# An SSD scan with a maxout FFN on one core: operand parts in three steps, queued steps two per unit, the maxima's parts on VectorE, and the last output in two stages

## The chip, the core and the metric

The kernel runs on one core of a Trainium2 chip. The core has TensorE (matrix products into PSUM), VectorE, ScalarE and GpSimd, each with its own queue of instructions worked off in order, and SyncE, whose queue here issues transfers. The engines wait for one another by semaphores. The metric is the device time of one execution in microseconds (us). In the profile PE is TensorE, PEld its loading of weights, DVE is VectorE, ACT is ScalarE, POOL is GpSimd and SP is SyncE.

## The reference

For 4 batches, 8 heads, 768 positions, head width 32 and state width 16, the first half is a scan with decays, written in chunks of positions:

```python
log_a = np.log(np.clip(a, 1e-06, 1.0))
cum = np.cumsum(la, axis=-1)                       # la: log_a of one chunk
L = np.exp(cum[..., :, None] - cum[..., None, :]) * causal
y_intra = ((C_c @ B_c^T) * L) @ x_c
y_inter = (C_c @ state) * np.exp(cum)
state = exp(sum(la)) * state + (B_c * exp(cum[-1] - cum))^T @ x_c
```

The heads are then put side by side (3072 tokens of 256 values) and go through a maxout layer and an output layer:

```python
h = np.maximum(np.maximum(x @ w1, x @ w2), x @ w3)  # 256 -> 768
return (h @ w_out).astype(np.float32)               # 768 -> 256
```

All is float32, and float32 accuracy is wanted.

## The kernel before

**Tiling.** The kernel takes 128 positions of all four batches at a time: six blocks (c = 0 to 5) of 512 tokens. For each block the scan makes the scores (L559, one group for batches 0 and 1 and one for batches 2 and 3), weights them by the decays (`scan_weight`, L567, on VectorE), and adds the old state's part (L582) and the block's own (L595). The decays are exponentials on ScalarE (L460, four heads per `part`), of a table L that comes by DMA and is masked on GpSimd (L453). `scan_c` (L501) makes C's transposed form, `scan_cd` (L512) the decayed one, from a bank of PSUM that it thereby sets free.

**The layer.** The three weights of the first layer, in 9 pieces of 256 columns, and the output weight, in 3 pieces, are 12 "weights". They arrive as raw words (`fetch`), are decoded into floats (`decode`: L208 and L217 on ScalarE, L209 and L212 on VectorE, L218 on GpSimd; `sign`: L221 on VectorE), and block 0 uses these whole floats (L657, L761). Blocks 1 to 5 use another form: every operand is split into parts, a high one, a low one and a scaled difference, in a type with faster products, and three products stand for one: the difference's product (L701 for the first layer), scaled by −KAPPA in the bank by ScalarE (L687), and then the high and the low part's products on top of it (L718). `weight_parts` makes a weight's parts, `scan_y` those of y, and `hidden` those of a maximum: high part on ScalarE (L636), low part by a subtraction on GpSimd (L637; on VectorE for the last two maxima only), difference on VectorE (L630).

**Units.** A block's first layer is 18 units (9 weights k, two halves g). A unit makes L718 for its bank and opens the bank two units ahead (L701, L687), in a ring of four banks; VectorE copies the result (L723) or takes the maximum (L725). A maximum is done after three weights; its parts are started one unit later and finished another unit later (`after`). With all six maxima of a block done, the "down" products with the output weight (L766) follow, listed in `downs`: for each half of the batches first Y (the difference's products, then scaled) and then X (the other two). They are issued in the middle of the next block's units, at places that the tables X1 to X3 and Y1 to Y3 set with a "D".

**Order.** The program is written out by hand; each engine gets its instructions in the order of the calls. Steps of the scan that would hold up VectorE are put in a list, `later`, and `pop(1)` after each unit releases one of them. In the loop over block 0's 18 groups (n) and in block 1's units, the weights are decoded and split step by step; W1 says which split starts at which k. The parts of the last three weights are finished at the end of block 1 (`finals`), because the buffers are those that block 0's down products read.

**Pools.** Scores, transposes, y, states and outputs share a ring of four banks (`att_bank`).

Of the kernel before, what the change touches and what calls it, by code (L numbers as in the profile page):

```python
# [20 lines left out]
def kernel(  # L21
# [218 lines left out]
    def weight_parts(k):  # L240
# [6 lines left out]
        def last():  # L247
# [13 lines left out]
    splitting = []

    def split(k=None):

        for step in splitting:
            step()
        del splitting[:]
        if k is not None:
            a, b, *splitting[:] = weight_parts(k)
            a()  # L270
            b()
# [420 lines left out]
    AHEAD = 2  # L692
# [13 lines left out]
    def unit():  # L706
# [35 lines left out]
    downs, outs, finals = [], {}, {}  # L742
# [4 lines left out]
    def down_next():  # L747
# [9 lines left out]
        for b in bs:  # L757
# [13 lines left out]
            if what == "X" and c == NC - 1:  # L771
                put(c, o, (b,))
        if what == "Y":
            down_scaled(o)
        elif c < NC - 1 and (c > 0 or bs[0] % 2):
            put(c, o, (2 * a, 2 * a + 1))

    def put(c, o, bs):

        ob = ffn.tile([P, 2, DM], FP32, tag="ob", name="ob")  # L780
        part = slice(bs[0] % 2, bs[-1] % 2 + 1)
        nc.scalar.activation(  # L782
            ob[:, part], o[:, part], AF.Copy, scale=(1.0 + TAU) ** 2 if c else 1.0)
        (nc.scalar if c == NC - 1 else nc.sync).dma_start(
            out=out.rearrange("(b s) m -> s b m", s=S)[c * P:(c + 1) * P, bs[0]:bs[-1] + 1],
            in_=ob[:, part])
# [99 lines left out]

    for n in range(NF * 3):
# [85 lines left out]
    for c in range(1, NC):  # L973
# [3 lines left out]
        for k in range(NW):  # L977
            unit()
            pop(1)
            if c == 1:  # L980
                if k < 2:
                    sign()
                if k == 0:
                    decode()
                if k < 4:
                    split(W1[k])
                elif W1[k]:
                    *steps, finals[W1[k]] = weight_parts(W1[k])
                    for step in steps:
                        step()  # L990
# [21 lines left out]
            pop(1)  # L1012
# [13 lines left out]
        if c == 1:  # L1026
# [35 lines left out]
```

## Time and profile before

| | us |
|---|---|
| median of 3 runs (341.5 to 345.76) | 342.2 |
| the profiled execution | 341.14 |
| its span, first to last instruction | 339.4 |

| engine | busy us | share of the span | instructions |
|---|---|---|---|
| TensorE | 294.3 | 87% | 2054 |
| VectorE | 177.2 | 52% | 264 |
| ScalarE | 183.3 | 54% | 409 |
| GpSimd | 126.2 | 37% | 112 |

The mean granted clock of TensorE is 0.94 of full speed. Busy shares are means over stages that differ, so the stages have to be read one by one; a wait is the bracket at a row's end, with the time that the engine stood idle before the instruction and what it waited for. A row's time is counted from the span's start.

### The profile page before, as it was taken

Reading aid. Unit: us, or ns where it says so; the run is one execution under the profiler, and the core shown is the slowest. Engines: PE = TensorE matmul, PEld = TensorE weight load, DVE = VectorE, ACT = ScalarE, POOL = GpSimd, SP = SyncE. Lnnn points to the kernel's source line nnn. Section 1 sums busy time; section 2 is a strip of 40 time slices with the busy share of each in tenths; the row PEclk is TensorE's granted clock in tenths of the full one; section 3 lists DMA queues with packets and bytes.
Section 4 is the critical chain, followed back from the end, with each engine's and each line's share of the span. In section 5 each row is a group of like instructions: output and inputs, shape, how many; then the busy total and the mean of one; then the engine's idle time right before and its main releaser. Section 6 shows DMA issues by size and latency. Waiting matters only on the chain.

```text
span 339.4 us, 5409 instructions
## 1 busy us (share of the span) xinstructions
PE 294.3 (87%) x2054; PEld 222.0 (65%) x2054; DVE 177.2 (52%) x264; ACT 183.3 (54%) x409; POOL 126.2 (37%) x112
## 2 busy tenths in 40 slices
PE   7899949969698499699799999799999899999765
PEld 4664324646465387498478798477897576887564
DVE  2758766965336434421837722767614467426810
ACT  2965956847847646625447755466845144245221
POOL 4346695669744701900507401434303032012100
PEclk9999987999959789979969999989999799999979
DMA  7979799989070003902703902600000000010001
GB/s 86 281 236 318 132 161 273 199 167 167 32 91 3 0 2 101 234 8 78 77 2 100 210 3 86 69 2 2 0 33 32 0 2 1 2 62 0 2 0 62
DMA packets 105049, 28.13 MB, mean 83 GB/s; under 512 B 75328, under 2 KB 101952, under 8 KB 105024
## 3 DMA queue, kind: packets, MB, share of 16 engines
q1 hardware_dynamic: 104144, 27.14, 39.6%
q10 hardware_dynamic: 880, 0.66, 0.6%
q8 instruction: 16, 0.26, 0.3%
q14 instruction: 9, 0.07, 0.1%
HBM read 24.54 MB, written 3.24 MB: 82 GB/s over the span
## 4 chain that ended last, share of the span: by engine, by line
PE 53%; DVE 16%; issue 13%; POOL 11%; ACT 5%; POOLq 0%; ACTq 0%
PE up L718 13%; PE o L766 12%; PE up L701 9%; PE up L657 5%; PE s L559 4%; DVE h L630 4%; POOL wd L250 3%; POOL wp L256 3%; DVE m L723 3%; DVE m L725 3%; POOL L L453 2%; PE y L595 2%; DVE L L567 2%; ACT L L460 2%; DVE six L623 1%
## 5 line engine op out<-in xcount | busy, mean ns | idle before, releaser
L718 PE MATMUL up<-six,wp 128*128 128x512 f32 x360 | 102.1, 412 | 0.4 <-ACT up L687 0.3
L637 POOL TENSOR_TENSOR h<-m,h 128x512 fp32r<-128x512 f32 x28 | 35.9, 1286 | 150.0 <-ACT h L636 149.6
L718 PEld LDWEIGHTS up<-six,wp 128*128 128x128 f32 x360 | 71.5, 200 | 18.5 <-ACT up L687 2.7
L725 DVE TENSOR_TENSOR m<-m,up 128x512 f32<-128x512 f32 x60 | 41.0, 684 | 80.7 <-PE up L718 80.3
L687 ACT ACTIVATE up<-up 128x512 f32<-128x512 f32 x90 | 51.2, 582 | 54.6 <-PE up L701 54.5
L701 PE MATMUL up<-six,wd 128*128 128x512 f32 x180 | 62.0, 432 | 6.4 <-DVE six L630 5.8
L460 ACT ACTIVATE L<-L,ncums 128x128 f32<-128x128 f32 x160 | 50.2, 390 | 3.5 <-POOL L L453 3.5
L701 PEld LDWEIGHTS up<-six,wd 128*128 128x128 f32 x180 | 33.1, 201 | 19.3 <-DVE six L630 8.0
L559 PE MATMUL s<-six,six 32*128 32x256 f32 x192 | 26.2, 456 | 16.9 <-DVE L L567 7.2
L723 DVE COPY m<-up 128x512 f32<-128x512 f32 x30 | 20.6, 688 | 34.1 <-PE up L718 33.3
L630 DVE SCALAR_TENSOR_TENSOR h<-h,h 128x512 fp32r<-128x512 f32 x30 | 33.6, 1121 | 7.7 <-POOL h L637 7.6
L559 PEld LDWEIGHTS s<-six,six 32*128 32x128 f32 x192 | 15.0, 203 | 26.4 <-issue 12.3
L766 PE MATMUL o<-wp,h 128*128 128x256 f32 x240 | 31.2, 287 | 1.0 <-ACT ob L782 1.0
L657 PE MATMUL up<-six,w 128*128 128x512 f32 x64 | 31.3, 635 | 0.7 <-ACT wp L258 0.5
L766 PEld LDWEIGHTS o<-wp,h 128*128 128x128 f32 x240 | 30.4, 195 | 1.7 <-ACT ob L782 1.4
L567 DVE TENSOR_TENSOR L<-s,L 128x512 f32<-128x512 f32 x46 | 30.4, 680 | 0.0
L766 PE MATMUL o<-wd,h 128*128 128x256 f32 x120 | 18.8, 304 | 7.4 <-DVE h L630 6.4
L453 POOL TENSOR_SCALAR_AFFINE_SELECT L<-L 128x1024 f32<-128x1024 f32 x20 | 24.7, 1259 | 0.0
L766 PEld LDWEIGHTS o<-wd,h 128*128 128x128 f32 x120 | 17.3, 207 | 9.5 <-DVE h L630 7.3
L657 PEld LDWEIGHTS up<-six,w 128*128 128x128 f32 x64 | 12.4, 203 | 16.9 <-issue 12.6
L636 ACT ACTIVATE h<-m 128x512 fp32r<-128x512 f32 x30 | 18.7, 624 | 8.8 <-DVE m L725 8.8
L218 POOL TENSOR_TENSOR six<-six 128x512 uint32<-128x512 uint32 x12 | 15.3, 1271 | 20.9 <-DVE six L212 10.5
(93 smaller groups left out, 294.4 us busy)
## 6 DMA issues: line engine op xcount, KB each, us to landing
L<-cums SPq DMA_DIRECT2D x10, 1024.0 KB, 8.9
rb<-in_moe_w_dram SPq DMA_DIRECT2D x9, 512.0 KB, 6.4
raw_x<-in_x_dram SPq DMA_DIRECT2D x6, 512.0 KB, 10.9
out_dram<-ob SPq DMA_DIRECT2D x10, 256.0 KB, 2.1
raw_B<-in_B_dram SPq DMA_DIRECT2D x6, 256.0 KB, 4.5
raw_C<-in_C_dram SPq DMA_DIRECT2D x6, 256.0 KB, 6.4
rb<-in_moe_w_out_dram SPq DMA_DIRECT2D x3, 512.0 KB, 5.1
E<-cums SPq DMA_DIRECT2D x40, 32.0 KB, 2.2
```

The lines of the kernel that those rows point to most:

```text
L453: nc.gpsimd.affine_select(out=Ls[c][:, b], in_=Ls[c][:, b], pattern=[[0, NH], [1, P]], compare_op=ALU.is_ge, fill=MASKED, base=0, channel_ ...
L460: nc.scalar.activation(L[:, b, h], L[:, b, h], AF.Exp, bias=ncum[c][:, b * NH + h:b * NH + h + 1], scale=1.0)
L559: nc.tensor.matmul(out=s[:, i].rearrange("j g i -> j (g i)"), lhsT=st["BT"][rows, b], rhs=st["CT"][rows, :, b], start=(i == 0), stop=True, ...
L567: nc.vector.tensor_tensor(out=M, in0=s, in1=M, op=ALU.mult)
L630: nc.vector.scalar_tensor_tensor(out=out, in0=lo.bitcast(FP32), scalar=-1.0 / TAU, in1=hi.bitcast(FP32), op0=ALU.mult, op1=ALU.add)
L637: (nc.vector if soon else nc.gpsimd).tensor_tensor(out=lo, in0=src, in1=hi.bitcast(FP32), op=ALU.subtract)
L657: nc.tensor.matmul(out=bank, lhsT=whole[3 * (f // 2) + i][:, k, f % 2 * P:(f % 2 + 1) * P], rhs=yT[0][:, k], start=(k == 0), stop=(k == KD ...
L687: nc.scalar.activation(bank, bank, AF.Copy, scale=-KAPPA)
L701: nc.tensor.matmul(out=o, lhsT=weight_part(k, 2, kk, cols), rhs=yT[c][2][:, kk], start=(kk == 0), stop=(kk == KD - 1), skip_group_check=True)
L718: nc.tensor.matmul(out=o, lhsT=weight_part(k, j, kk, cols), rhs=yT[c][j][:, kk], start=False, stop=(kk == KD - 1 and j == 1), skip_group_c ...
L725: nc.vector.tensor_tensor(out=m[g], in0=m[g], in1=o, op=ALU.max)
L766: nc.tensor.matmul(out=o[:, b % 2], lhsT=hs[f][p][:, tokens(b)], rhs=weight_part(NW + f // 2, p, f % 2, slice(0, DM)), start=(first and p ...
```

## The change

**Weights' parts.** ScalarE now makes both scaled copies of a weight one behind the other (the high part in `lo`'s place, and the high part times TAU in `hi`'s), then GpSimd subtracts, then GpSimd makes the difference. All parts are smaller by TAU than before, and the output's scale, BACK, makes up for it in both layers. The steps are called by number (`split(k, step, ...)`): W0 sets them for weights 0 to 3 in the loop over n, W1 now for weights 4 to 11 in block 1's units (the copies in the unit's first half, the two GpSimd steps in its second); `finals` is gone. The decoding of weights is moved to other n, earlier, and ends in the loop.

**Queued steps.** `pop(1)` after each unit becomes `pop(2)`.

**Maxima.** The subtraction of `hidden` is on VectorE for all 30 maxima, and is made with the difference, a unit later than before. In the last block the parts of the last but one maximum are made behind the last unit.

**Output.** Block 0's four down products move: one ahead of block 1, three to k = 1, 3 and 4. For the last block, `last_down` takes a bank for each batch, with the high and low parts' products in one half and the difference's in the other; it first goes through four of the six hidden pieces for all batches and then through the last two; ScalarE and VectorE put the halves together, and SP issues the stores.

```diff
+    BACK = ((1.0 + TAU) / TAU) ** 2
...
         return [
-            lambda: nc.scalar.activation(hi, w, AF.Copy, scale=HIGH),
+            lambda: (nc.scalar.activation(lo, w, AF.Copy, scale=HIGH),
+                     nc.scalar.activation(hi, w, AF.Copy, scale=HIGH * TAU)),
             lambda: nc.gpsimd.tensor_tensor(
-                out=lo, in0=w, in1=hi.bitcast(FP32), op=ALU.subtract),
-            lambda: nc.scalar.activation(lo, lo.bitcast(FP32), AF.Copy, scale=1.0 / TAU),
+                out=lo, in0=w, in1=lo.bitcast(FP32), op=ALU.subtract),
             last]
...
-    def hidden(f, src, soon):
+    def hidden(f, src):
         hs[f] = hi, lo, d = [hidden_place(f, j, F32R) for j in range(3)]
         nc.scalar.activation(hi, src, AF.Copy, scale=HIGH)
-        (nc.vector if soon else nc.gpsimd).tensor_tensor(
-            out=lo, in0=src, in1=hi.bitcast(FP32), op=ALU.subtract)
         def rest():
+            nc.vector.tensor_tensor(out=lo, in0=src, in1=hi.bitcast(FP32), op=ALU.subtract)
             difference(d, hi, lo)
...
             if last:
-                start()
+                if g == 1:
+                    ends[0]()
+                    start()
+                else:
+                    ends.append(start)
...
+    def last_down():
+        c = NC - 1
+        os_ = [att_bank([P, 2, DM], "o") for _ in range(NB)]
+        for fs in (range(NF - 2), range(NF - 2, NF)):
+            for b, o in enumerate(os_):
+                for f in fs:
+                    for p in (2, 0, 1):
+                        nc.tensor.matmul(
+                            out=o[:, p // 2], lhsT=hs[f][p][:, tokens(b)],
+                            rhs=weight_part(NW + f // 2, p, f % 2, slice(0, DM)),
+                            start=(f == 0 and p == 2), stop=(f == NF - 1 and p > 0),
+                            skip_group_check=True)
+                if fs[-1] == NF - 1:
+                    ob = ffn.tile([P, 2, DM], FP32, tag="ob", name="ob")[:, 0]
+                    nc.scalar.activation(ob, o[:, 0], AF.Copy, scale=BACK)
+                    nc.vector.scalar_tensor_tensor(
+                        out=ob, in0=o[:, 1], scalar=-KAPPA * BACK, in1=ob, op0=ALU.mult,
+                        op1=ALU.add)
+                    nc.sync.dma_start(
+                        out=out.rearrange("(b s) m -> s b m", s=S)[c * P:(c + 1) * P, b], in_=ob)
...
+    signs, decodes = (0, 2, 3, 5, 7, 8, 10, 12, 14, 15, 17), (0, 2, 3, 5, 7, 8, 10, 12, 14, 15)
+    W0 = {11: (0, 0), 12: (0, 1), 13: (0, 2, 1, 0), 14: (1, 1), 15: (1, 2, 2, 0), 16: (2, 1),
+          17: (2, 2, 3, 0)}
...
-        if g == 0 and n <= 16:
+        if n in signs:
             sign()
-            if n <= 14:
-                decode()
+        if n in decodes:
+            decode()
...
-        if n > 6:
-            split((n - 7) // 2 if n % 2 else None)
+        if n in W0:
+            split(*W0[n])
...
+    downs += [(0, "0", b) for b in range(NB)]
+    down_next()
     pop(9)
+    split(3, 1)
     transposed(2, False)
-    downs += [(0, "0", b) for b in range(NB)]
+    split(3, 2)
-    X1 = ["tc", "", "D", "s0", "", "s2", "y", "AD", ""]
-    Y1 = ["", "", "D", "", "", "", "", "D", ""]
+    X1 = ["tc", "D", "", "s0", "D", "s2", "y", "A", ""]
+    Y1 = ["", "", "", "D", "", "", "", "", ""]
-    W1 = [6, 7, 8, None, 9, 10, 11, None, None]
+    W1 = [4, 5, 6, 7, 8, 9, 10, 11, None]
...
             unit()
-            pop(1)
+            pop(2)
...
-        if c == 1:
-            for k in range(NW, NW + 3):
-                finals[k]()
         downs += [(c, "Y", 0), (c, "Y", 1), (c, "X", 0), (c, "X", 1)]
-    while downs:
-        down_next()
+    last_down()
```

Three places show how instructions move. The first is ScalarE in block 0's loop, ahead of the first scores of block 1 (rb is a raw weight, w a decoded one, wp two of its parts, six a buffer); before:

```order
L255 ACTIVATE wp<-w 128x512
L208 ACTIVATE six_532<-rb 128x512
L217 ACTIVATE six_532<-rb 128x512
L258 ACTIVATE wp<-wp 128x512
L460 ACTIVATE L<-L,ncums 128x128 x4
L482 COPY six_555<-trB 128x512
L501 ACTIVATE six_563<-trC,parity 128x512 x2
```

and now:

```order
L210 ACTIVATE six_531<-rb 128x512
L219 ACTIVATE six_531<-rb 128x512
L459 ACTIVATE L<-L,ncums 128x128 x4
L481 COPY six_551<-trB 128x512
L500 ACTIVATE six_559<-trC,parity 128x512 x2
L257 ACTIVATE wp<-w 128x512
L258 ACTIVATE wp<-w 128x512
```

The copies that the scores need stood behind a split step that reads what GpSimd wrote; now two decode steps stand there (of weight 8, before of weight 7), and the splits come behind.

The second is VectorE in block 3's units, at the scores (m is a running maximum, up a unit's bank, s a scores' bank, h a part of a finished maximum); before:

```order
L725 TENSOR_TENSOR m<-m,up 128x512 x3
L567 TENSOR_TENSOR L<-s,L 128x2x256
L723 COPY m<-up 128x512
L630 SCALAR_TENSOR_TENSOR h_2_1951<-h_1_1950,h_0_1949 128x512
L567 TENSOR_TENSOR L<-s,L 128x2x256
L723 COPY m<-up 128x512
L630 SCALAR_TENSOR_TENSOR h_2_1968<-h_1_1967,h_0_1966 128x512
L567 TENSOR_TENSOR L<-s,L 128x2x256
L725 TENSOR_TENSOR m<-m,up 128x512
L567 TENSOR_TENSOR L<-s,L 128x2x256
```

and now:

```order
L723 TENSOR_TENSOR m<-m,up 128x512 x3
L566 TENSOR_TENSOR L<-s,L 128x2x256 x2
L721 COPY m<-up 128x512
L638 TENSOR_TENSOR h_1_1950<-m,h_0_1949 128x512
L629 SCALAR_TENSOR_TENSOR h_2_1951<-h_1_1950,h_0_1949 128x512
L566 TENSOR_TENSOR L<-s,L 128x2x256 x2
L721 COPY m<-up 128x512
L638 TENSOR_TENSOR h_1_1968<-m,h_0_1967 128x512
L629 SCALAR_TENSOR_TENSOR h_2_1969<-h_1_1968,h_0_1967 128x512
```

All four weightings of the first scores' banks now stand ahead of the second copy, with one subtraction more ahead of the last two of them.

The third is GpSimd in block 1's units, behind the third masks (wd is a weight's third part); before:

```order
L453 AFFINE_SELECT L<-L 128x1024 x2
L256 TENSOR_TENSOR wp<-w,wp 128x512
L637 TENSOR_TENSOR h_1_1060<-m,h_0_1059 128x512
L637 TENSOR_TENSOR h_1_1077<-m,h_0_1076 128x512
L256 TENSOR_TENSOR wp<-w,wp 128x512
L453 AFFINE_SELECT L<-L 128x1024 x2
L637 TENSOR_TENSOR h_1_1259<-m,h_0_1258 128x512
L543 TENSOR_TENSOR old<-S,E 128x256
L546 TENSOR_TENSOR S<-S,old 128x256
L250 TENSOR_TENSOR wd<-wp 128x512 x3
L637 TENSOR_TENSOR h_1_1294<-m,h_0_1293 128x512
```

and now:

```order
L452 AFFINE_SELECT L<-L 128x1024 x2
L259 TENSOR_TENSOR wp<-w,wp 128x512
L252 TENSOR_TENSOR wd<-wp 128x512
L259 TENSOR_TENSOR wp<-w,wp 128x512
L252 TENSOR_TENSOR wd<-wp 128x512
L452 AFFINE_SELECT L<-L 128x1024 x2
L542 TENSOR_TENSOR old<-S,E 128x256
L545 TENSOR_TENSOR S<-S,old 128x256
L259 TENSOR_TENSOR wp<-w,wp 128x512
L252 TENSOR_TENSOR wd<-wp 128x512
```

The maxima's subtractions are gone from GpSimd's queue, and the last weights' third parts come in pairs with the second ones, not three in a row at the end.

## Rows read from the trace of the kernel before

**Rows 1.** Windows by stage: stretch, length, busy and instructions per engine, clock, DMA.
```profile
0.00:72.92 72.92, 59.87 (x477) 34.34 (x477) 49.61 (x83) 46.77 (x101) 44.98 (x46) 0.95 0.98 206
72.92:135.01 62.09, 51.80 (x322) 38.79 (x321) 27.80 (x40) 39.46 (x98) 30.02 (x25) 0.89 0.33 61
135.01:190.94 55.93, 49.28 (x349) 38.81 (x350) 26.79 (x38) 28.58 (x67) 21.42 (x19) 0.91 0.47 98
190.94:239.42 48.48, 45.15 (x349) 36.39 (x349) 26.57 (x38) 28.12 (x67) 15.63 (x13) 0.96 0.29 44
239.42:286.71 47.29, 44.37 (x317) 35.83 (x317) 25.75 (x37) 22.23 (x47) 7.72 (x6) 0.96 0.04 12
286.71:319.72 33.01, 32.70 (x176) 27.70 (x176) 17.29 (x23) 14.24 (x27) 6.46 (x6) 1.00 0.05 17
319.72:339.40 19.68, 11.14 (x73) 10.13 (x71) 3.37 (x5) 3.87 (x8) 0.00 (x0) 0.91 0.08 27
```

**Rows 2.** Timeline of TensorE: start, us, instruction, idle before and its releaser.
```profile
50.01 2.09 PE L559 MATMUL s<-six,six 32*128 32x256 f32 x16 [4.71 <-ACT six L501]
```

**Rows 3.** Timeline of ScalarE ahead of it.
```profile
46.53 0.63 ACT L258 ACTIVATE wp<-wp 128x512 fp32r<-128x512 f32 x1 [4.69 <-POOL wp L256]
```

**Rows 4.** Windows at and behind idle times, columns as in rows 1.
```profile
115.00:121.00 6.00, 6.00 (x94) 5.02 (x95) 1.03 (x2) 3.74 (x11) 2.46 (x3) 0.51 0.01 3
141.00:144.30 3.30, 0.41 (x2) 0.22 (x2) 1.65 (x2) 0.51 (x2) 2.67 (x3) 1.00 1.33 178
144.30:148.20 3.90, 3.90 (x14) 3.32 (x15) 1.12 (x2) 1.16 (x2) 0.00 (x0) 0.56 0.13 15
168.30:176.00 7.70, 7.69 (x55) 5.25 (x55) 1.78 (x3) 2.34 (x6) 0.00 (x0) 0.56 0.01 2
218.30:223.00 4.70, 4.67 (x20) 3.52 (x21) 1.06 (x2) 0.79 (x2) 0.00 (x0) 0.66 0.00 0
```

**Rows 5.** DMA issues of 35.2 to 37.7: size, us to landing.
```profile
rb<-in_moe_w_dram SPq DMA_DIRECT2D x1, 512.0 KB, 6.1
```

**Rows 6.** Groups by line, TensorE, block 1: count, busy, mean ns, idle and releasers.
```profile
L761 PE MATMUL o<-w,h 128*128 128x256 f32 x48 | 11.0, 379 | 0.0
L559 PE MATMUL s<-six,six 32*128 32x256 f32 x32 | 5.4, 505 | 4.0 <-DVE six L512 1.8 <-ACT ob L782 1.5 <-DVE L L567 0.7
...
L582 PE MATMUL y<-six,S 32*64 32x128 f32 x32 | 2.4, 405 | 5.2 <-DVE L L567 5.1
```

**Rows 7.** GpSimd by line in block 1, then its and TensorE's timeline in block 2.
```profile
L256 POOL TENSOR_TENSOR wp<-w,wp 128x512 fp32r<-128x512 f32 x6 | 8.6, 1439 | 6.8 <-ACT wp L255 6.8
...
137.19 4.21 POOL L250 TENSOR_TENSOR wd<-wp 128x512 fp32r<-128x512 f32 x3
...
144.27 1.50 PE L766 MATMUL o<-wd,h 128*128 128x256 f32 x7 [2.44 <-DVE h L630]
```

**Rows 8.** Groups by line, TensorE, block 3.
```profile
L701 PE MATMUL up<-six,wd 128*128 128x512 f32 x36 | 12.2, 426 | 0.8 <-DVE six L630 0.8
...
L559 PE MATMUL s<-six,six 32*128 32x256 f32 x32 | 4.5, 417 | 2.5 <-DVE L L567 2.4
```

**Rows 9.** Timeline of VectorE in block 3, and its groups by line there.
```profile
210.37 0.69 DVE L725 TENSOR_TENSOR m<-m,up 128x512 f32<-128x512 f32 x1 [5.64 <-PE up L718]
...
212.33 1.52 DVE L630 SCALAR_TENSOR_TENSOR h<-h,h 128x512 fp32r<-128x512 f32 x1
...
217.50 0.68 DVE L567 TENSOR_TENSOR L<-s,L 128x512 f32<-128x512 f32 x1
...
L630 DVE SCALAR_TENSOR_TENSOR h<-h,h 128x512 fp32r<-128x512 f32 x6 | 7.1, 1187 | 0.0
```

**Rows 10.** Timelines of TensorE and VectorE in the tail.
```profile
330.52 3.14 PE L766 MATMUL o<-wp,h 128*128 128x256 f32 x24 [0.52 <-ACT ob L782]
334.14 1.69 PE L766 MATMUL o<-wp,h 128*128 128x256 f32 x12 [0.47 <-ACT ob L782]
...
320.30 0.69 DVE L637 TENSOR_TENSOR h<-m,h 128x512 fp32r<-128x512 f32 x1 [0.76 <-ACT h L636]
```

More of the change, by code (lines that the diff above doesn't have):

```diff
@@ L254, in weight_parts, with split @@
         return [
-            lambda: nc.scalar.activation(hi, w, AF.Copy, scale=HIGH),
+            lambda: (nc.scalar.activation(lo, w, AF.Copy, scale=HIGH),
+                     nc.scalar.activation(hi, w, AF.Copy, scale=HIGH * TAU)),
             lambda: nc.gpsimd.tensor_tensor(
-                out=lo, in0=w, in1=hi.bitcast(FP32), op=ALU.subtract),
-            lambda: nc.scalar.activation(lo, lo.bitcast(FP32), AF.Copy, scale=1.0 / TAU),
+                out=lo, in0=w, in1=lo.bitcast(FP32), op=ALU.subtract),
             last]
[L261 to L271, printed above, removed]
+    jobs = {}
+    def split(*pairs):
+        for k, step in zip(pairs[::2], pairs[1::2]):
+            if step == 0:
+                jobs[k] = weight_parts(k)
+            jobs[k][step]()
     def weight_part(k, j, row, cols):
@@ L691 @@
     opened, m, ready = {}, {}, set()
-    AHEAD = 2
+    AHEAD, ends = 2, []
     def unit_open(u):
@@ L731, in start @@
             def start(f=2 * q + g, src=m[g]):
-                rest = hidden(f, src, last)
+                rest = hidden(f, src)
                 if last:
@@ L737, in unit @@
             if last:
-                start()
+                if g == 1:
[3 more added lines that the diff above has]
+                    ends.append(start)
             else:
                 after(1, start)
-    downs, outs, finals = [], {}, {}
+    downs, outs = [], {}
     def tokens(b):
@@ L770, in down_next @@
                         skip_group_check=True)
-            if what == "X" and c == NC - 1:
-                put(c, o, (b,))
         if what == "Y":
             down_scaled(o)
-        elif c < NC - 1 and (c > 0 or bs[0] % 2):
+        elif c > 0 or bs[0] % 2:
             put(c, o, (2 * a, 2 * a + 1))
@@ L780, in put @@
         ob = ffn.tile([P, 2, DM], FP32, tag="ob", name="ob")
[L781 to L786, printed above, removed]
+        nc.scalar.activation(ob, o, AF.Copy, scale=BACK if c else 1.0)
+        nc.sync.dma_start(
+            out=out.rearrange("(b s) m -> s b m", s=S)[c * P:(c + 1) * P, bs[0]:bs[-1] + 1], in_=ob)
+    def last_down():
[16 more added lines that the diff above has]
+                        op1=ALU.add)
+                    nc.sync.dma_start(
+                        out=out.rearrange("(b s) m -> s b m", s=S)[c * P:(c + 1) * P, b], in_=ob)
     for b in range(2, NB):
@@ L944 @@
             scores(1, 2)
-        if n == 17:
-            decode()
-        if n > 6:
-            split((n - 7) // 2 if n % 2 else None)
+        if n in W0:
+            split(*W0[n])
     shared["ffn"] = False
@@ L978 @@
             unit()
-            pop(1)
-            if c == 1:
[L981 to L990, printed above, removed]
+            pop(2)
+            if c == 1 and W1[k]:
+                split(W1[k], 0)
             part(n, ds[k][0])
@@ L1011 @@
             unit()
-            pop(1)
+            pop(2)
+            if c == 1 and W1[k]:
+                split(W1[k], 1, W1[k], 2)
             if n < NC and k == 0:
@@ L1025 @@
         pop(9)
-        if c == 1:
-            for k in range(NW, NW + 3):
-                finals[k]()
         downs += [(c, "Y", 0), (c, "Y", 1), (c, "X", 0), (c, "X", 1)]
-    while downs:
-        down_next()
+    last_down()
 _INS = ['x', 'a', 'B', 'C', 'moe_w1', 'moe_w2', 'moe_w3', 'moe_w_out']
```

## Prediction

> **What bounds the kernel now.** I first read the stretches by stage [rows 1]. Times count from the span's start; block c is positions c·128 to c·128+127 of all four batches, and a stage begins with the first L718 of its block. TensorE is the busiest engine in every stage, but the stages differ: blocks 3, 4 and 5 take 48.48, 47.29 and 33.01 us, block 1 takes 62.09, and block 2 takes 55.93 for the same work as block 3. The last 19.68 us hold only 11.14 us of TensorE work. Then I looked for what ended TensorE's idle times, and at its granted clock behind them: after a long idle time it is near 0.5 (1.2 GHz instead of 2.4) for some microseconds [rows 4]. So a wait is paid twice, and I price both: the idle time, and (1 − granted clock) × the stretch behind it.
>
> The waits: in front, the first scores of block 1 start 4.71 us late, behind ScalarE's L501 [rows 2], which stood in ScalarE's queue behind an L258 that waited 4.69 us for GpSimd [rows 3]. In block 1 the scores L559 wait 4.0 us, 3.3 of it for banks that L512 and L782 release, and the old-state product L582 waits 5.2 us for L567 [rows 6]. In block 2 the down product waits 2.44 us for the maxima's parts, while GpSimd runs three L250 in a row [rows 7]. In block 3 the second scores wait 2.4 us for L567, and the next block's first products 0.8 us for L630 [rows 8]; blocks 2 and 4 have the same order. At the end TensorE works 11.14 of 19.68 us, and the last products wait 0.52 and 0.47 us for L782 [rows 10].
>
> **The change, part by part, against the profiled time of 341.14 us** (span 339.40 and 1.74 around it; the median of the runs shown is 342.2, 1.1 more).
>
> *Front.* Each of 12 weights still takes two ScalarE and two GpSimd operations, but ScalarE no longer waits for GpSimd between its two, and the first split now stands behind the copies of L501, where it stood ahead. What is late next: decoding moves forward, so L208 for weight 8 stands ahead of these copies and waits for its transfer, issued after 35.2 and landed 6.1 us later, at 41.3 or a little after [rows 5]. ScalarE was free from 46.53 − 4.69 = 41.84, so this costs next to nothing. From the end of the wait to the scores passed 50.01 − 46.53 = 3.5 us; the two decode steps in place of one split step add about 1. So the scores start at 41.8 + 3.5 + 1 = 46.3: −3.7. Ends: −1 (the transfers take the rest) and −4.7. Behind the scores ScalarE has two decodes more to do before block 1, so I count nothing for the clock. One of block 0's four down products moves into TensorE's wait for the parts of y; its time is counted in the next term.
>
> *Block 1.* GpSimd is busy 30.0 of 62.09 us [rows 1]. It loses five L637 and one decode, and makes eight whole splits where it made six L256 and four L250: at 1.44 and 4.21 / 3 = 1.40 [rows 7] six more, at most 38.5 us if nothing is taken off. ScalarE is busy 39.46; three split steps more at 0.63 [rows 3], two decode steps less: 40. Both stay below the stage. Removed: L582's wait of 5.2, since no L637 on GpSimd stands ahead of L630 and L567, and two queued steps leave per unit; the clock behind it, 0.49 × 6.0 = 2.9 [rows 4]; 0.7 of L559's wait, the part for L567; one down product, a quarter of L761's 11.0 us [rows 6], less its pipeline's tail, 2.4. Kept: the 3.3 us at the first scores and the clock behind them. Their last bank is that of trC, released by L512, which still comes behind a copy and the parts of the first maximum; these wait for ScalarE's L636, which stands behind eight exponentials as before. Sum −11.2, so the stage is 50.9. Ends: −5 (half of it comes back as waits for ScalarE) and −19.5 (all idle time, 10.3, all clock, 0.11 × 62.09 = 6.8, and the down product).
>
> *Block 2.* Removed: 2.9 us idle from 141.0 to 144.3, since the splits are done in block 1 and VectorE makes the parts, and 0.44 × 3.9 = 1.7 of clock; the second scores' 2.4 and 0.44 × 7.7 = 3.4 of clock [rows 4]; 0.8 at the boundary, since the five queued steps behind y leave in three pops instead of five, and the next block's products open during the last units. Sum 11.2.
>
> *What remains of the second scores' wait.* VectorE's queue, from the last maximum ahead of L567, now holds it, two L567, a copy, a pair, two L567, and TensorE waits for these four L567 only. A pair is the subtraction, 0.69 on VectorE [rows 10], and an L630, as long where GpSimd is quiet. From 210.37 [rows 9] that is 0.69 + 1.36 + 0.69 + 1.38 + 1.36 = 5.5, until 215.9. Before, the fourth L567 ended at 217.50 + 0.68 = 218.2, behind two copies, two L630 of up to 1.52 and a maximum. The wait of 2.4 shrinks by 2.3; with a margin for the engines' hand-over I leave 0.8, and assume that the clock stays (if it falls, 3.4 in block 2 and 1.6 in block 3 come back). Block 2: −10.4; ends −5 and −11.2.
>
> *Blocks 3 and 4.* Block 3: 2.4 + 0.34 × 4.7 [rows 4] + 0.8 = 4.8, less 0.8: −4.0. Block 4 has 2.92 idle against 3.33, and the same clock [rows 1]: −3.5. The subtractions add 6 × 0.69 = 4.1 us to VectorE, which is busy 26.57 of 48.48 in block 3: its slack of 20 us hides them, and without that cover they would cost the 4.1. Ends for both together: +2 and −8.8.
>
> *Block 5.* 0.31 idle [rows 1]: 0.
>
> *Tail.* The 72 down products stay, but 48 now run before the last two maxima are needed. At 3.14 / 24 = 0.131 us [rows 10] these take 6.3; a maximum, ScalarE's step and four VectorE steps at 0.69 take 4.1, which is hidden. 72 × 0.131 = 9.4; then, as before behind the last product, 339.40 − 335.83 = 3.6; and one VectorE step more, at most 0.69. That is 13.7 against 19.68: −6.0; ends −4 (the clock falls) and −7. The stores now go through SP's queue, which has nothing else left.
>
> Queues passed: on SP the second output store of block 0 moves ahead of block 3's E, B and C; it falls in the middle of block 1, and these are used a stage later.
>
> Sum: −3.7 − 11.2 − 10.4 − 4.0 − 3.5 − 6.0 = −38.8, so 341.1 − 38.8 = **302.3 us**.
>
> **A rule against it.** [Rows 9] show an L630 of 1.52 us, with GpSimd at work; L637, of the same shape and also with two inputs from SBUF, takes 0.69 at the end, where GpSimd does nothing [rows 1, 10]. The Trainium skill ("SBUF — State Buffer", Who interferes with whom) says that a VectorE instruction with two SBUF inputs and a GpSimd instruction that reads SBUF shut each other out for the whole instruction; the trace agrees in direction. The Trainium skill ("Perfetto Trace Analysis", Optimizing Scalar/DVE Operations) warns that moving work between these two might therefore not help; no run so far shows the moved subtraction beside a split. By that rule the time would be that of rival B.
>
> **Rivals.**
> A. *The middle waits stay*: the pairs make VectorE so late that the second scores wait 2.4 us as before in three blocks. Then block 2 gives −5.4 and blocks 3 and 4 −0.8 each: 341.1 − 3.7 − 11.2 − 5.4 − 1.6 − 6.0 = 313.2. Against it: the order of the queue above.
> B. *VectorE is held by GpSimd in block 1*, where GpSimd works over half the time. Six pairs, twelve operations, each held by 1.52 − 0.69 = 0.83: 10 us, most of it ahead of L512 and L567; 10 of the 11.2 come back: 312.3. Against: VectorE is busy 27.80 of 62.09 there.
> C. *Slower: the pairs set the pace of the units.* A unit is some 1.3 us of TensorE (block 5 less 72 products of 0.131, over 18 units); a pair with both halves held is 3.0 on VectorE, 1.8 more than L630's mean of 1.19 [rows 9]. If all 28 moved pairs are held and on TensorE's path, that is 50 us: 352.7. It needs 1.7 us per pair (47 us) to be slower by over 2%. Against: in blocks 2 to 5 GpSimd has little left but four masks a block.
> D. *Only the tail gains*: the other waits move and do not go (front to the transfers, block 1 to ScalarE, the second scores as before): 341.1 − 6.0 = 335.1.
>
> **Chances.** Forecast 0.62, A 0.14, B 0.13, D 0.08, C 0.03. The forecast's terms all at their good ends give 341.1 − 51.2 = 290, all at their poor ends 328; six terms do not all go one way, and A and B lie at 312 and 313. I take 291 to 318, which leaves out C, D and the far ends. A measurement of this kernel tells about 2% from no change. Faster by over 2% (under 335): 0.92; within 2%: 0.05; slower: 0.03.
>
> **What would show it.** The stages again: block 1 starting near 69 us and 51 long, block 2 45, blocks 3 and 4 44 each, block 5 33, tail 14. Front: right if the first scores start near 46. Block 1: right if L582 waits under 1 us and ScalarE never for GpSimd's split; wrong if the subtractions average over 1.2 us. Middle: right if the second scores wait under 1 us at a clock of 1.00. End: right if TensorE has no gap from the last unit to its last product. The prediction is wrong if block 1 stays above 58 us, or a new wait of over 3 us stands in blocks 2 to 4.

## The result

The changed kernel takes 320.56 us (median of 4 runs, 320.1 to 327.11) where the kernel before takes 343.98 (341.5 to 346.37): a ratio of 0.9315 [0.9214, 0.9417], faster. The forecast was 302.3 with a range up to 318, so the sign is right and the size is not: of 38.8 us expected, 20.6 came (341.14 to 320.50, the two profiled executions). In the profiles of e_tail, e_ready, e_two, e_best, e_best2 and e_best3 below TensorE ran at half clock from about 17 to 27 us, in block 0, which lengthens the front by some 3 to 5 us; these fronts are not compared with the others.

The changed kernel's stages, in the same columns as [rows 1] (a stage begins with the block's first L716):

```profile
0.00:71.05 71.05, 60.08 (x488) 36.59 (x489) 50.21 (x87) 46.15 (x100) 38.78 (x42) 0.98 0.99 204
71.05:128.85 57.80, 47.23 (x310) 35.27 (x310) 27.87 (x40) 38.78 (x97) 32.75 (x29) 0.88 0.54 111
128.85:178.19 49.34, 44.89 (x349) 35.96 (x348) 31.52 (x45) 29.09 (x70) 9.64 (x8) 0.97 0.40 78
178.19:226.03 47.84, 43.36 (x350) 34.75 (x349) 31.54 (x45) 28.11 (x67) 8.38 (x7) 1.00 0.24 35
226.03:271.06 45.03, 42.62 (x318) 34.22 (x316) 27.34 (x44) 22.86 (x47) 0.00 (x0) 1.00 0.04 13
271.06:305.00 33.94, 32.95 (x175) 27.62 (x174) 19.18 (x30) 14.08 (x25) 0.00 (x0) 1.00 0.05 16
305.00:318.80 13.80, 8.80 (x73) 8.58 (x71) 4.97 (x9) 2.80 (x6) 0.00 (x0) 0.96 0.11 38
```

The third busy time is VectorE's: in block 3 it rises from the 26.57 of [rows 1] to 31.54, while GpSimd's, the fifth, falls from 15.63 to 8.38. Every stage but block 5 is shorter than before, yet each is longer than forecast: block 1 by 6.9 us, 2 by 3.8, 3 by 3.3, 4 by 1.2, the front by 1.9.

What TensorE waits for now (its timeline; in brackets the idle time ahead of the instruction and what ended it):

```profile
46.21 1.15 PE L558 MATMUL s<-six,six 32*128 32x256 f32 x16 [2.62 <-ACT six L500]
...
60.98 0.43 PE L581 MATMUL y<-six,S 32*64 32x128 f32 x4 [3.51 <-DVE L L566]
...
95.52 4.62 PE L763 MATMUL o<-w,h 128*128 128x256 f32 x12 [2.80 <-DVE L L566]
...
136.16 1.42 PE L768 MATMUL o<-wd,h 128*128 128x256 f32 x7 [2.04 <-DVE h L629]
...
156.37 2.12 PE L558 MATMUL s<-six,six 32*128 32x256 f32 x16
...
266.64 0.50 PE L699 MATMUL up<-six,wd 128*128 128x512 f32 x1 [1.32 <-DVE m L723]
...
267.96 0.49 PE L699 MATMUL up<-six,wd 128*128 128x512 f32 x1 [0.83 <-DVE six L629]
```

The first row answers [rows 2]: the scores start at 46.21, where 46.3 was forecast. The fifth answers the scores' row of [rows 8]: all 16 pass without a wait. The third is new: a down product of block 0 right behind the first scores, whose bank they still hold; it comes while the clock is already low, so that 12 products take 4.62 us. The last two stand at the end of block 4. At this place [rows 8] had one wait of 0.8 in block 3, for L630, a step of y; that one is still there (0.83, for L629), and a wait of 1.32 for a maximum has come ahead of it, at the end of each of blocks 2 to 4: 2.15 us together.

In block 4 GpSimd does nothing (0.00 above). So the two waits there are VectorE's own. Its queue ahead of them, y's parts being L622 and L629 with six:

```profile
263.25 0.68 DVE L638 TENSOR_TENSOR h<-m,h 128x512 fp32r<-128x512 f32 x1
263.96 0.69 DVE L629 SCALAR_TENSOR_TENSOR h<-h,h 128x512 fp32r<-128x512 f32 x1
264.57 0.68 DVE L622 TENSOR_TENSOR six<-y,six 128x512 fp32r<-128x512 f32 x1
265.29 0.69 DVE L629 SCALAR_TENSOR_TENSOR six<-six,six 128x512 fp32r<-128x512 f32 x1
265.90 0.68 DVE L723 TENSOR_TENSOR m<-m,up 128x512 f32<-128x512 f32 x1
```

The maximum L723 at 265.90 frees the bank that the opening product wants. A pair and two of y's steps stand ahead of it, without a gap.

In block 2 the pairs (a maximum's subtraction L638 and its difference L629) are also held: they take longer while GpSimd works. VectorE, and beside it GpSimd:

```profile
130.56 1.52 DVE L638 TENSOR_TENSOR h<-m,h 128x512 fp32r<-128x512 f32 x1
132.12 1.46 DVE L629 SCALAR_TENSOR_TENSOR h<-h,h 128x512 fp32r<-128x512 f32 x1
133.50 0.68 DVE L721 COPY m<-up 128x512 f32<-128x512 f32 x1
134.11 0.97 DVE L638 TENSOR_TENSOR h<-m,h 128x512 fp32r<-128x512 f32 x1
135.11 0.99 DVE L629 SCALAR_TENSOR_TENSOR h<-h,h 128x512 fp32r<-128x512 f32 x1
```

```profile
130.44 1.10 POOL L516 TENSOR_TENSOR raw_B<-raw_B,from_js 128x512 f32<-128x512 f32 x1 [0.32 <-PE trB L485]
131.49 3.04 POOL L452 TENSOR_SCALAR_AFFINE_SELECT L<-L 128x1024 f32<-128x1024 f32 x2
134.50 1.05 POOL L542 TENSOR_TENSOR old<-S,E 128x256 f32<-128x256 f32 x1
```

The subtraction that takes 0.68 in block 4 takes 1.52 here. The copy L721 at 133.50, which has one input and that from a bank, takes 0.68 beside the same masks. The down product needs the second pair: it is the wait of 2.04 at 136.16. The forecast had taken 2.9 us of waits away at this place in block 2 and put none into block 3, where the same wait of 2.04 is new.

### The profile page after: what moved, and what is told of

It is laid out like the page before. It is cut to its first block, busy times and chain, and to the rows that moved or that the text cites. A ratio compares the mean times of both kernels' runs of the same rounds, so it can differ in the third digit from the quotient of the medians.

```text
span 318.8 us, 5385 instructions
## 1 busy us (share of the span) xinstructions
PE 279.9 (88%) x2054; PEld 213.0 (67%) x2054; DVE 192.6 (60%) x296; ACT 181.9 (57%) x407; POOL 89.6 (28%) x84
## 4 chain that ended last, share of the span: by engine, by line
PE 60%; DVE 23%; DMA 6%; ACT 4%; POOL 3%; issue 2%; SPq 0%; POOLq 0%; ACTq 0%
PE up L716 20%; PE up L699 11%; PE o L768 11%; PE s L558 5%; DVE h L629 4%; DVE h L638 4%; DMA raw_C<-in_C_dram 3%; DVE m L721 3%; PE o L763 3%; POOL six L220 3%; DVE w L223 2%; PE o L793 2%; PE y L594 2%; DMA rb<-in_moe_w_out_dram 2%; DVE six L629 2%
## 5 line engine op out<-in xcount | busy, mean ns | idle before, releaser
L716 PE MATMUL up<-six,wp 128*128 128x512 f32 x360 | 98.8, 398 | 0.0
L723 DVE TENSOR_TENSOR m<-m,up 128x512 f32<-128x512 f32 x60 | 40.9, 685 | 73.5 <-PE up L716 73.1
L716 PEld LDWEIGHTS up<-six,wp 128*128 128x128 f32 x360 | 69.2, 192 | 15.5 <-ACT up L685 0.2
L721 DVE COPY m<-up 128x512 f32<-128x512 f32 x30 | 20.6, 687 | 22.5 <-PE up L716 22.5
L566 DVE TENSOR_TENSOR L<-s,L 128x512 f32<-128x512 f32 x46 | 29.3, 682 | 0.7 <-ACT L L459 0.7
L655 PE MATMUL up<-six,w 128*128 128x512 f32 x64 | 28.8, 598 | 0.1
L558 PE MATMUL s<-six,six 32*128 32x256 f32 x192 | 20.9, 412 | 7.9 <-ACT six L500 4.0
L638 DVE TENSOR_TENSOR h<-m,h 128x512 fp32r<-128x512 f32 x30 | 26.0, 868 | 0.7 <-ACT h L635 0.7
L629 DVE SCALAR_TENSOR_TENSOR h<-h,h 128x512 fp32r<-128x512 f32 x30 | 25.4, 846 | 1.0
L768 PE MATMUL o<-wp,h 128*128 128x256 f32 x192 | 24.3, 283 | 0.0
L768 PEld LDWEIGHTS o<-wp,h 128*128 128x128 f32 x192 | 23.9, 192 | 0.3
L558 PEld LDWEIGHTS s<-six,six 32*128 32x128 f32 x192 | 12.5, 184 | 15.3 <-ACT six L500 5.0
L545 POOL TENSOR_TENSOR S<-S,old 128x256 f32<-128x256 f32 x4 | 2.9, 734 | 69.7 <-DVE S L537 69.7
L259 POOL TENSOR_TENSOR wp<-w,wp 128x512 fp32r<-128x512 f32 x12 | 15.4, 1284 | 15.5 <-ACT wp L257 15.5
```

The costliest lines, as they stand in the source:

```text
L558: nc.tensor.matmul(out=s[:, i].rearrange("j g i -> j (g i)"), lhsT=st["BT"][rows, b], rhs=st["CT"][rows, :, b], start=(i == 0), stop=True, ...
L566: nc.vector.tensor_tensor(out=M, in0=s, in1=M, op=ALU.mult)
L629: nc.vector.scalar_tensor_tensor(out=out, in0=lo.bitcast(FP32), scalar=-1.0 / TAU, in1=hi.bitcast(FP32), op0=ALU.mult, op1=ALU.add)
L638: nc.vector.tensor_tensor(out=lo, in0=src, in1=hi.bitcast(FP32), op=ALU.subtract)
L655: nc.tensor.matmul(out=bank, lhsT=whole[3 * (f // 2) + i][:, k, f % 2 * P:(f % 2 + 1) * P], rhs=yT[0][:, k], start=(k == 0), stop=(k == KD ...
L716: nc.tensor.matmul(out=o, lhsT=weight_part(k, j, kk, cols), rhs=yT[c][j][:, kk], start=False, stop=(kk == KD - 1 and j == 1), skip_group_c ...
```

## The experiments

Twelve kernels, each beside runs of the kernel before. Stages in us, from the profiled executions (the last column is block 5 and the tail). All go by the first product L716 of a block, or the line that stands for it; [rows 1] cut blocks 3 to 5 of the kernel before 0.17 us behind it, so two numbers of the first row differ by that:

| kernel | front | block 1 | block 2 | block 3 | block 4 | 5, tail |
|---|---|---|---|---|---|---|
| before | 72.92 | 62.09 | 55.76 | 48.48 | 47.29 | 52.86 |
| forecast | 69.2 | 50.9 | 45.5 | 44.5 | 43.8 | 46.7 |
| changed | 71.05 | 57.80 | 49.34 | 47.84 | 45.03 | 47.74 |
| e_pool | 71.36 | 55.26 | 45.86 | 44.68 | 43.53 | 46.81 |
| e_bpop2 | 72.41 | 58.93 | 53.84 | 44.72 | 43.56 | 52.64 |
| e_pop2tail | 72.70 | 58.92 | 53.84 | 44.72 | 43.52 | 47.10 |
| e_pairs | 72.41 | 55.08 | 47.28 | 47.83 | 45.02 | 47.78 |

**e_tail**: the kernel before with the new last output (`last_down()` for the loop over `downs`, and `ends`).

> The kernel before with the two-stage sum of the last output alone. If the tail's gain stands by itself, it is the difference of the two tails, 19.68 - 13.81 = 5.9 us: 335.3 where the kernel before is 341.2, a ratio near 0.983, and the stages ahead of the tail keep their lengths. If the gain hangs on the other parts (the clock in the tail, or late third parts of the weights), the tail stays above 16 us and the ratio above 0.99.

340.5 us (335.57 to 340.79), ratio 0.9875 [0.9742, 1.0007]: by the whole time unclear, since the front of the profiled run was 78.1 us. By stages it is clear: block 5 and tail take 47.12 instead of 52.86, and blocks 1 to 4 are those of before within 0.1. The tail's gain stands by itself.

**e_pop1**: the change with one queued step per unit.

```diff
-            pop(2)
+            pop(1)
```

> The changed kernel with one queued step per unit in place of two. If the release of two steps pays for the middle blocks, as I forecast, the second scores wait 2 us or more again with a half clock behind it in blocks 2 to 4 and the old-state product waits in block 1, while the waits of 1.3 and 0.8 us at the boundaries shrink to 0.8: 320.5 + 3 x 4 + 3 - 3 x 1.3 = about 332, ratio to before near 0.973. If the pairs on VectorE alone made the middle's gain and the two steps only cost at the boundaries, 316 (0.927).

340.59 us (337.44 to 344.84), ratio 0.9943 [0.989, 0.9997]: nearly the whole gain is gone, more than either theory said. Blocks 3 and 4 take 52.2 and 50.0 us, 3.7 and 2.7 more than before the change. TensorE at block 3's second scores:

```profile
214.81 0.67 PE L558 MATMUL s<-six,six 32*128 32x256 f32 x2 [1.86 <-DVE L L566]
```

With the pairs on VectorE and one step per unit the change gains next to nothing.

**e_pool**: the change with the maxima's subtraction back on GpSimd, issued at once.

```diff
+        nc.gpsimd.tensor_tensor(out=lo, in0=src, in1=hi.bitcast(FP32), op=ALU.subtract)
         def rest():
-            nc.vector.tensor_tensor(out=lo, in0=src, in1=hi.bitcast(FP32), op=ALU.subtract)
             difference(d, hi, lo)
```

> The changed kernel with the maxima's subtraction back on GpSimd, issued at once as before. If GpSimd's queue was the late one in block 1 (my step), the old-state product and the first scores wait 3 us or more again there, and block 1 is 5 us longer or more: 326 or above (ratio 0.955 or above). If instead VectorE held by GpSimd is what ate block 1's and block 2's gain (rival B), the held pairs go and the kernel becomes 314 or less (0.92).

313.16 us (309.19 to 314.14), ratio 0.9111 [0.9015, 0.9207] against 0.9315 for the whole change. My step for GpSimd's queue fell: the old-state product of block 1, which I had freed by taking the subtractions off GpSimd, does not wait here either. Its stages in blocks 2 to 4:

```profile
126.62:172.48 45.86, 43.04 (x349) 34.57 (x348) 25.71 (x39) 29.15 (x70) 16.76 (x14) 1.00 0.44 86
172.48:217.16 44.68, 42.74 (x350) 34.53 (x348) 25.59 (x39) 28.11 (x67) 15.43 (x13) 1.00 0.28 41
217.16:260.69 43.53, 42.03 (x317) 34.00 (x316) 24.66 (x38) 22.75 (x47) 8.01 (x6) 1.00 0.04 13
```

GpSimd works nearly twice as long as in the changed kernel in blocks 2 and 3; TensorE never waits for it in these blocks, and VectorE once, 1.03 us for a subtraction in block 2. The end of block 4 again, VectorE and then TensorE:

```profile
253.64 0.68 DVE L629 SCALAR_TENSOR_TENSOR h<-h,h 128x512 fp32r<-128x512 f32 x1
254.24 0.68 DVE L622 TENSOR_TENSOR six<-y,six 128x512 fp32r<-128x512 f32 x1
254.96 0.69 DVE L629 SCALAR_TENSOR_TENSOR six<-six,six 128x512 fp32r<-128x512 f32 x1
255.56 0.68 DVE L724 TENSOR_TENSOR m<-m,up 128x512 f32<-128x512 f32 x1
```

```profile
256.30 0.50 PE L700 MATMUL up<-six,wd 128*128 128x512 f32 x1 [0.57 <-DVE m L724]
```

One subtraction less in the row, 0.68 us, and the wait for the maximum is 0.57 instead of 1.32; the one for y's L629 behind it stays (0.82).

**e_ready**: two empty steps in the queue, so that the next block's first opening product comes one unit later.

```diff
-        later.append(lambda: ready.add(c))
+        later.extend([lambda: None, lambda: None, lambda: ready.add(c)])
```

> The changed kernel with two empty steps in the queue ahead of the one that says that y's parts are there, so that the next block's first opening product stands one unit later in TensorE's order; nothing else moves. If the boundary waits (1.31 + 0.82 us in blocks 2 to 4, 0.50 + 0.82 in block 1) come from opening too early, they go to under 0.5 us a boundary and the kernel gains 4 to 7 us: 313.5 to 316.5, ratio near 0.915. If TensorE then waits as long at the same place for the same banks, no change: 320.5 (0.9315).

324.98 us (320.19 to 326.03), ratio 0.9415 [0.9294, 0.9537]. Blocks 2 to 4 take 48.84, 48.87 and 44.45 us, 142.2 together as in the changed kernel. But that sum hides two things: at the same clock (0.97 and 1.00) blocks 2 and 4 are 0.5 and 0.6 us shorter, and block 3 is 1.0 longer with a clock of 0.97 instead of 1.00. At the end of block 3 TensorE still waits:

```profile
227.87 0.50 PE L699 MATMUL up<-six,wd 128*128 128x512 f32 x1 [0.41 <-DVE m L723]
229.19 1.33 PE L699 MATMUL up<-six,wd 128*128 128x512 f32 x3 [0.82 <-DVE six L629]
```

The wait for the maximum fell from 1.31 to 0.41, the one for y's L629 stayed at 0.82. So opening too early is a part of the boundary's wait, worth some 0.9 us of it and half a microsecond of a block, not the 4 to 7 us expected; the rest is VectorE's queue.

**e_nomask**: the change without GpSimd's masks in blocks 2 and 3 (`if c == 1 and k in ks ...`); it leaves out that part of the result.

> The changed kernel without GpSimd's masks of blocks 4 and 5 (they stand in blocks 2 and 3; that part of the result is left out), so that GpSimd is nearly idle beside the maxima's pairs there. If GpSimd holds the pairs (rival B's mechanism, outside block 1), the pairs of 1.46 to 1.53 us ahead of the down product fall to about 0.7, its waits of 2.04 us in blocks 2 and 3 go to 0.7 or less as in block 4, and the two blocks become 2 us shorter each: 316.5. If VectorE is late by its own work and order alone, the waits stay at 2 and the time at 320.5.

320.79 us (317.76 to 322.67), ratio 0.938 [0.9289, 0.9471]; the whole time tells nothing here, the stages do: blocks 2 and 3 take 46.91 and 46.80, 2.4 and 1.0 us less, and block 4 45.01 as in the changed kernel. VectorE in block 2, and the down product:

```profile
131.37 1.52 DVE L638 TENSOR_TENSOR h<-m,h 128x512 fp32r<-128x512 f32 x1
132.93 0.69 DVE L629 SCALAR_TENSOR_TENSOR h<-h,h 128x512 fp32r<-128x512 f32 x1
...
134.14 0.68 DVE L638 TENSOR_TENSOR h<-m,h 128x512 fp32r<-128x512 f32 x1
```

```profile
136.01 1.10 PE L768 MATMUL o<-wd,h 128*128 128x256 f32 x7 [1.09 <-DVE h L629]
```

Its stage, block 2:

```profile
129.64:176.55 46.91, 43.38 (x349) 34.73 (x348) 29.00 (x45) 29.03 (x70) 3.72 (x4) 1.00 0.41 81
```

The first L638 still runs beside L516 (1.10 us from 131.24) and takes 1.52; those that had the masks beside them fall from 1.46 and 0.97 to 0.69 and 0.68. So GpSimd does hold the pairs. The down product's wait falls from 2.04 to 1.09 and 0.98, not to 0.7, about 2 us in the two blocks. The other 1.5 of their 3.5 us is block 2's clock, 1.00 instead of 0.97: in the changed kernel it fell behind the wait of 2.04 in block 2 and not behind the same wait in block 3, so this share is partly luck. It is not all: e_pool is 1.1 and 2.1 us shorter still.

**e_two**: the change with two places moved.

```diff
-    X1 = ["tc", "D", "", "s0", "D", "s2", "y", "A", ""]
-    Y1 = ["", "", "", "D", "", "", "", "", ""]
+    X1 = ["tc", "D", "", "s0", "DD", "s2", "y", "A", ""]
+    Y1 = ["", "", "", "", "", "", "", "", ""]
...
-        room = six((1, 2, 5)[n % 3] if n < 10 else 2)
+        room = six((1, 2, 5)[n % 3])
```

> The changed kernel with two places moved: in block 1 the third down product of block 0 one unit later, beside the fourth; in front the twelfth weight decoded in another scratch buffer than the eleventh. If the down product behind the first scores' banks made block 1's new wait, the 2.80 us go, and half of the 10 us at half clock behind it: block 1 is 52 to 55 us instead of 57.8. If the shared scratch made the front late, the 2.40 us of ScalarE and most of the 3.5 us at the old-state product go: the front is 69 us instead of 71.05. Both: 313 to 316. If block 1 is held by VectorE's backlog wherever the product stands, it stays at 57 and the whole at 318.5 to 320.5.

318.54 us (317.11 to 320.69), ratio 0.9302 [0.9212, 0.9391]. Block 1 takes 52.97 us instead of 57.80, as expected; the whole missed its 313 to 316. The moved down products:

```profile
99.30 5.42 PE L763 MATMUL o<-w,h 128*128 128x256 f32 x24 [0.41 <-DVE L L566]
```

Its wait went from 2.80 to 0.41, and 24 products take 5.42 where 12 took 4.62: the clock is back by then. In front the old-state product waits 2.10, where it waits 3.51 in the changed kernel and 2.9 in e_pool, e_pop1 and e_nomask, whose front has the old scratch too. But from the first scores to block 1 it is 25.6 us against 24.8; the front's miss isn't settled by this.

**e_bpop2**: the kernel before with `pop(2)` for `pop(1)`, nothing else.

> The kernel before with two queued steps per unit, nothing else. If the release by two pays in the middle with the subtractions on GpSimd, as it seems to with the new splits, the second scores' waits of 2.4 us and their half clock go: blocks 2 to 4 lose 4 to 6, 3 and 3 us, block 1 some 2, and the whole is 326 to 331 (ratio 0.955 to 0.97). If it pays only together with splits done in block 1, or with pairs on VectorE, 336 to 341 (0.985 to 1).

326.08 us (325.94 to 327.85), ratio 0.9528 [0.9452, 0.9604], so this edit of one character, twice, gives 13.3 of the 20.6 us between the profiled executions (341.14 to 327.85), and by the medians 15.7 (341.8 to 326.08). Blocks 3 and 4, and the end of block 3:

```profile
185.18:229.90 44.72, 42.81 (x350) 34.51 (x348) 25.27 (x39) 27.93 (x66) 14.68 (x13) 1.00 0.23 34
229.90:273.46 43.56, 42.03 (x317) 34.01 (x316) 24.64 (x38) 22.75 (x47) 7.99 (x6) 1.00 0.04 13
...
225.47 0.50 PE L701 MATMUL up<-six,wd 128*128 128x512 f32 x1 [0.77 <-DVE m L725]
```

The clock is 1.00 (0.96 in [rows 1]), and TensorE's time, 44.37 to 42.03 in block 4, falls with it. Both blocks are shorter than in the changed kernel. The last row is a wait that the kernel before does not have: the release of two steps brings it, with no subtraction on VectorE.

**e_pop2tail** and **e_pairs**: to e_bpop2 the new tail is added; then, in e_pairs, the subtractions on VectorE (`rest` as in the change). Splits and places of before in both.

> The kernel before with two of the change's parts, two queued steps per unit and the two-stage sum at the end. If these two add up as they were measured apart (326.1 with the first, 5.9 less in the tail with the second), 320 to 321: the same as the whole change, so that all its other parts together bring nothing. If they share a gain, 323 or more.

> The same, and the maxima's subtractions moved to VectorE into the step a unit later, with the weights' parts made as before. If moving them costs by itself (held pairs, and VectorE's own time in the units), as the comparison with them put back says, 5 to 11 us more than without: 326 to 331. If it costs only beside the changed kernel's splits in block 1, at most 2 us more: 320 to 322. If it gains where GpSimd is busy with splits, as I forecast for blocks 1 and 2, under 319.

322.98 us (322.5 to 326.44), ratio 0.9519 [0.9443, 0.9595], and 319.52 (317.08 to 323.07), ratio 0.936 [0.9282, 0.9437]. The first is the sum of its parts by the stages: against e_bpop2 the span falls from 326.1 to 320.8 us, and block 5 and tail by 5.5 (the medians, 326.08 and 322.98, show 3.1). The second lies between the last two cases by its median, and the stages show why; blocks 2 and 3:

```profile
127.49:174.77 47.28, 43.39 (x350) 34.73 (x348) 30.96 (x45) 29.10 (x70) 7.91 (x8) 1.00 0.63 131
174.77:222.60 47.83, 43.36 (x349) 34.72 (x348) 31.54 (x45) 28.11 (x67) 8.38 (x7) 1.00 0.25 35
```

Against e_pop2tail in the table, moving the subtractions gains 3.8 and 6.6 us in blocks 1 and 2, where GpSimd has splits ahead of them ([rows 7]: three L250, 4.21 us), and costs 3.1, 1.5 and 0.7 in blocks 3, 4 and 5, where it has not. With the new splits, which are done earlier, the same move costs in every one of these blocks: changed less e_pool is 2.5, 3.5, 3.2, 1.5 and 0.9 us.

**e_best**: e_pool and e_two together.

> The changed kernel with the maxima's subtractions back on GpSimd and the same two places moved. If the three losses are separate, 309.2 - 1.8 (front) - 3 to 5 (block 1) = 303 to 305 us, near the forecast, with stages near 69.5, 51, 46, 44.5, 43.5 and 46.7. If the moves only pass the wait on, 308 to 313.

309.32 us (308.87 to 310.25), ratio 0.9031 [0.8961, 0.91], not the 303 to 305 of separate losses. Block 1 takes 52.02, blocks 2 to 4 45.8, 44.7, 43.8. The moved down product keeps a gain of 3.2 us in block 1; with a front as in e_pool the span would be 2.6 us shorter.

**e_best2**: e_best with block 2's exponential of E and its product Cd queued at k = 1 instead of 2 (`k == int(c == 1)`).

> The kernel with the subtractions back on GpSimd and the two places moved, and besides block 2's exponential of E with the product Cd queued one pair of units earlier in block 1, ahead of the first maximum's parts. If the first scores' wait of 4.74 us in block 1 is for that product behind the parts, as I took it when I kept it, the wait falls under 1 us, and with it part of the 10 us at half clock behind: block 1 is 45 to 48 us instead of 52.0, the whole 302 to 305. If the banks are late for another reason, 308 to 310 as without it.

310.05 us (308.26 to 311.38), ratio 0.9102 [0.9043, 0.916]; block 1 is 52.8. The first scores wait no more, so their wait was for Cd's place; but it is passed on. TensorE, GpSimd and VectorE behind the scores:

```profile
98.61 7.02 PE L764 MATMUL o<-w,h 128*128 128x256 f32 x24 [8.06 <-DVE L L566]
```

```profile
89.82 1.28 POOL L259 TENSOR_TENSOR wp<-w,wp 128x512 fp32r<-128x512 f32 x1
91.18 1.59 POOL L252 TENSOR_TENSOR wd<-wp 128x512 fp32r<-128x512 f32 x1
92.73 2.13 POOL L452 TENSOR_SCALAR_AFFINE_SELECT L<-L 128x1024 f32<-128x1024 f32 x2
94.83 1.25 POOL L637 TENSOR_TENSOR h<-m,h 128x512 fp32r<-128x512 f32 x1
```

```profile
96.12 1.74 DVE L629 SCALAR_TENSOR_TENSOR h<-h,h 128x512 fp32r<-128x512 f32 x1 [3.87 <-POOL h L637]
```

Here the subtraction on GpSimd is the late one: it stands behind a split and a mask, 5 us.

**e_best3**: e_best2 with block 1's first two subtractions on VectorE, 28 on GpSimd.

```diff
-                rest = hidden(f, src)
+                rest = hidden(f, src, c == 1 and q == 0)
```

> The last kernel with one difference: the subtractions of block 1's first two maxima on VectorE, the other 28 on GpSimd. If the down product's wait of 8.06 us there is for a subtraction that stands behind a split and a mask in GpSimd's queue (GpSimd 94.83, VectorE's next step waits 3.87 for it), the wait falls to 4 us or less and block 1 from 52.8 to 47 to 50; the whole is 303 to 306. If the time goes to the pairs held on VectorE, or the wait is passed on a second time, 307 to 310 as without it.

305.84 us (303.3 to 307.84), ratio 0.8951 [0.8886, 0.9017], the fastest here. Block 1 takes 49.69:

```profile
95.64 8.17 PE L770 MATMUL o<-w,h 128*128 128x256 f32 x24 [3.96 <-DVE L L566]
```

The wait is halved, as expected; what is left stands behind the two pairs on VectorE, of whose four steps three are held (1.44, 1.16 and 1.64 us).

## Why the prediction was wrong

*The release of two steps* is the change's main part, and its total came out: in blocks 3 and 4 e_bpop2 comes to 44.72 and 43.56, forecast 44.5 and 43.8, with the second scores unbroken and the clock at 1.00. That the total fits is in part luck, by two misses that cancel. The second scores and their clock gave more than forecast, since the 0.8 us left for them are not there; the boundary's 0.8, which was to vanish, became 0.77 and 0.83 at the end of block 3. *The tail* was right: 13.80 us, forecast 13.7.

*The step that failed* is "its slack of 20 us hides them, and without that cover they would cost the 4.1". VectorE has slack over a block, but none between a pair and the next maximum: there the queued steps of y or the scores stand as well, and a maximum frees a bank. Put back on GpSimd (e_pool), the subtractions leave blocks 2 to 4, block 5 and the tail within 0.4 us of the forecast; on VectorE they cost 9.1 us there, where I had put nothing. In block 4, with GpSimd idle, it is VectorE's own time alone (1.5 us); in blocks 2 and 3 the masks make 3.5 of the 6.6, 1.5 of it by the clock. Of the boundary's 2.15, 0.8 is the old wait for y, the release of two steps brings 0.6 to 0.8 (e_bpop2), and the pairs the other 0.5 to 0.7.

*The signs that I had named* did not catch it. The first scores start at 46.21, the old-state product of block 1 waits 0.16 us, its subtractions average 1.10, the second scores do not wait, TensorE has no gap at the end, block 1 is 57.80 (58 was the bound) and no new wait in blocks 2 to 4 is over 3 us. Nearly all of them look at waits that the change removes; the loss is in several new waits of 0.7 to 3.5 us each. *Rival A* had pairs that make VectorE late, and 313.2; they did, but at the down products and the boundaries, not at the second scores.

*Rival B* named the hold, at 312.3, but in block 1 and there at 10 us; its place was also blocks 2 and 3, and in block 1 the subtractions' whole price was 2.5, and the pairs' steps there take 2.6 us more than where GpSimd is quiet. The Trainium skill ("SBUF — State Buffer", Who interferes with whom) says that a VectorE instruction contends with GpSimd's reads when two of its inputs come from SBUF, and not when at most one does, outside its two-port modes. The trace agrees: 1.52 and 1.46 against 0.68 and 0.69 for a pair, and 0.68 for the copy beside the masks.

*Two parts cure the same wait.* In blocks 1 and 2 GpSimd was late for the maxima because splits stood ahead. The new splits and the move to VectorE each remove much of that; the forecast credited the move with it and did not ask what the splits do alone. In span, against e_pop2tail (320.8): the move alone gives 5.4 us (315.4); the splits, decodes and places alone 13.3 (e_pool, 307.5); both 2.0 (318.8).

*Block 1* missed by 6.9: 4.8 of it is the down product put behind the first scores' banks (e_two), which I had only counted as removed work. The 3.3 us at the first scores stayed, as forecast (3.62). Of the last 2, 1 is the subtractions' (52.97 in e_two, 52.02 in e_best).

*Front*: the scores started as forecast, 3.8 us earlier than before, but the last of block 1's exponentials, without which L566 can't free the scores' banks for the old-state product, came only 0.46 earlier. ScalarE, before:

```profile
62.53 1.26 ACT L460 ACTIVATE L<-L,ncums 128x128 f32<-128x128 f32 x4
```

and now, behind two decodes, of which by the profile one waits for a weight's transfer and one for the scratch buffer that both use:

```profile
53.93 0.68 ACT L210 ACTIVATE six<-rb 128x512 f32<-128x512 f32 x1 [1.82 <-DMA rb<-in_moe_w_out_dram]
...
58.74 0.66 ACT L210 ACTIVATE six<-rb 128x512 f32<-128x512 f32 x1 [2.40 <-DVE w L223]
...
62.07 1.26 ACT L459 ACTIVATE L<-L,ncums 128x128 f32<-128x128 f32 x4
```

With the scratch moved (e_two) neither wait is there and the stretch is no shorter, so what would be next, and how much of the 1.9 us over the forecast these two waits explain, stays open.

## What to carry to other kernels

An engine's free time over a stage does not price an instruction added to it: look at what stands behind that instruction in its queue, and whether a bank waits for it. Signs of being wrong should also stand where the change adds work, not only where it removes a wait. When two parts of a change remove the same wait, count it once, and price the second part as if the first were in. The cheapest line of a change may be its gain: one part at a time on the kernel before shows that in one run each.

## What the hardware showed

Both sides pay for the hold. Beside VectorE's pairs two masks took 3.04 us on GpSimd (131.49 in the changed kernel), with VectorE idle 2.13 (92.73 in e_best2), and a step of a pair up to 1.52 instead of 0.68. In block 1 of e_best2 a difference L629 beside the splits takes 1.74: the step that was left on VectorE is held too, so the move doubled the number of steps at risk.
